# A respaced job plan, a reordered first batch and filler matmuls in a fused attention and gated feed-forward kernel

## The chip, the cores and the metric

The kernel runs on one core of a Trainium2 chip. The metric is the device time of one execution in microseconds (us). The engines are TensorE (PE; its weight loads are PEld), VectorE (DVE), ScalarE (ACT), GpSimd (POOL) and SyncE (SP); SyncE here only issues DMA transposes (its queue is SPq in the profile), and GpSimd also issues the plain DMAs.

## The reference

Two stages, one fed by the other. First an attention over induced points, for each of 4 batches with x of 12416 x 128 and 32 inducing points I:

```python
def mab(q, kv):
    s = scale * (q @ kv.transpose(0, 2, 1))
    s = s - s.max(-1, keepdims=True)
    a = np.exp(s)
    a /= a.sum(-1, keepdims=True) + 1e-09
    return a @ kv
h = mab(I, x)          # (B, 32, 128)
return mab(x, h)       # (B, 12416, 128)
```

Then a gated feed-forward layer on the 49664 rows that come out, with two 128 x 1536 weights and one 1536 x 128:

```python
gate = 1.0 / (1.0 + np.exp(-(x @ w_gate)))
val = x @ w_val
return (gate * val @ w_out).astype(np.float32)
```

## The kernel before, in words

The second attention's output is never formed. Since it is a2 @ h, the kernel computes hw = h @ [w_gate, w_val] once a batch (a 32-row operand for each 128-column piece of the weights) and feeds the weights a2 (32 numbers a token) straight to the products with hw. The sigmoid is taken as tanh, 0.5 * (1 + tanh(z / 2)).

**Blocks.** The main loop (lines 698 to 723) runs over 97 blocks: 24 blocks of 512 tokens for each batch and a last one of the four batches' 128-token tails. A batch's x is cut in 6 chunks q of 2048 tokens, two chunks make a pair d = 0, 1, 2, which serves 8 blocks. A block goes through four steps k. In a step, TensorE fills two value pieces (`v_fill` into the tile "va") and one more ("vb"); VectorE multiplies each with the gate's tanh (`v_mul`, line 434, tiles "u"); TensorE multiplies the u of the step before with w_out (`out_mm`, line 450, tile "acc"). After a block's 12th `out_mm`, in step 0 of the next block, `out_store` copies acc (ScalarE, line 460), transposes it (SyncE's queue, line 462, tile "on") and stores it (GpSimd's queue, line 465).

**Gate pairs.** The gate's 12 pieces go as 6 pairs: `g_next` fills one pair (line 366, tile "g") and takes its tanh on ScalarE (line 421). They run ahead of the multiplies: `gwant` starts at LEADP, rises by one in each step and once more in the odd steps. The first chance of a step stands right behind the va fill, the second behind the vb fill. A pair or a value piece has 32 rows of operand; those named in PADG (pairs) and PADV (value pieces) are spread to 128 rows with zeros (`hw_pad`, GpSimd's copies at lines 259 and 263, tiles "hwp").

**Jobs for the next batch.** In step 2 of a block, in place of the second chance for a pair, `do_extra` runs at most one job, planned by hand with `put(n, ...)`: "s1" (scores of the inducing points for two chunks, and their exp, line 163), "s1t" (the tail's), "h" (a chunk's share of h, line 194 on; VectorE adds it to "hacc" at lines 218 and 220), "hfin" and "hw" (the batch's h and hw), "s2" (scores of a pair d against h). A job's tile comes from the same two-buffer PSUM pool as the gate pairs, and its matmuls stand in TensorE's order ahead of all later fills.

**Events.** `at(n, k, f)` puts work without TensorE at the start of step k of block n: `load_x` (GpSimd's queue, line 84, f32 to f16), `xT_dma` (a chunk's transpose, SyncE's queue, line 142), `a1_dma` (the transpose of an s1 result, line 170, tile "a1n"), and for each s2 job the chain of `rep_events`: `e2_dma` (transpose, line 285), `s2_sum` (GpSimd's row sums, line 302), `s2_rec` (VectorE's reciprocal, line 310), `a2_mul` in two halves (GpSimd, line 320), `rep_dma` in two halves (transposes, line 335, tile "rep"). "rep" is what the value and gate fills of the pair's 8 blocks read, its first half in the first four, its second in the last four.

The order on each engine and queue is the program's order; nothing overtakes. The loads of one batch go into 7 buffers, the x transposes of a batch into one of two large tiles.

**The head.** Batch 0 has no blocks ahead of it, so lines 489 to 561 do its first attention by itself: chunks are transposed on TensorE as they arrive (`xT_pe`, line 480), scored (`s1n_mm`, line 178), passed through exp (line 516) and summed (`h_mm`, lines 194 to 213); then hfin, the scores of the first four token groups, hw, and the first block's rep by way of TensorE (line 550). `warm` (line 139) issues matmuls of 512 columns on ones, whose result nobody reads.

Of the kernel before, what the change touches and what calls it, by code (L numbers as in the profile page):

```python
# [9 lines left out]
F16 = mybir.dt.float16  # L10
AF = mybir.ActivationFunctionType
# [4 lines left out]
P = 128  # L16
# [6 lines left out]
def kernel(  # L23
# [41 lines left out]
    def slot_g(name):  # L65
        return ps_g.tile([P, 2 * TOK], F32, tag="g", name=name)
# [62 lines left out]
    hTs = [pers.tile([P, M], F16, tag=f"hT{b}", name=f"hT_{b}") for b in range(B)]  # L129
    hws = [pers.tile([P, NP2, P], F16, tag=f"hw{b}", name=f"hw_{b}") for b in range(B)]  # L130

    PADG, PADV = (0, 3), (2, 5, 8, 11)
    pads = [pers.tile([P, 8, P], F16, tag=f"hwp{b}", name=f"hwp_{b}") for b in range(B)]
    for t_ in pads:
        nc.gpsimd.memset(t_[:], 0.0)
# [39 lines left out]
    def s1n_mm(ps, b, q, lo, hi):  # L175
        for tk in range(lo, hi):
            j, r = tk % 4, tk // 4
            nc.tensor.matmul(
                ps[:, ds((j * 4 + r) * M, M)], xTs[b][:, ds(q * QT + tk * P, P)], indT[:],
                start=True, stop=True,  # L180
            )
# [10 lines left out]
    def h_mm(ps, b, q, first, last, tail, ch=0, cs=P):  # L192
        for j in range(4):
            nc.tensor.matmul(  # L194
                ps[:, cs:cs + P], ones[:, 0:P], a1n[(b, q)][:, j, :],
                start=first and j == 0, stop=last and j == 3,
            )
            if tail and j == 0:
                nc.tensor.matmul(
                    ps[:, cs:cs + M], ones[:, 0:P], a1n[(b, "t")][:], start=False, stop=False  # L200
                )
        for j in range(4):
            for r in range(4):
                nc.tensor.matmul(
                    ps[r * M:(r + 1) * M, ch:ch + P],
                    a1_chunk(b, q, 4 * r + j),
                    xqs[(b, q)][:, ts(4 * r + j, P)],
                    start=first and j == 0,
                    stop=last and j == 3 and not (tail and r == 0),
                )  # L210
        if tail:
            nc.tensor.matmul(  # L212
                ps[0:M, ch:ch + P], a1n[(b, "t")][:], xtail[:, b, :], start=False, stop=last,
            )
# [23 lines left out]
    def hfin_dve(ps, b):  # L238
        nc.vector.tensor_tensor(out=hTs[b][:], in0=recs[b][:], in1=ps[:, 0:M], op=ALU.mult)
# [235 lines left out]
    def xT_pe(b, q):  # L475
        for half in range(2):
            ps = slot_g(f"xt_{b}_{q}_{half}")
            v = ps[:].bitcast(F16)
            for j in range(8):
                nc.tensor.transpose(  # L480
                    v[:, ts(j, P)], xqs[(b, q)][:, ts(8 * half + j, P)], ident[:]
                )
            dst = xTs[b][:, ds(q * QT + half * 8 * P, 8 * P)]
            if half:
                nc.vector.tensor_copy(out=dst, in_=v[:, 0:8 * P])
            else:
                nc.scalar.copy(out=dst, in_=v[:, 0:8 * P])
# [14 lines left out]
    s1t_exp(0, ps)  # L502

    hps = slot_a("h_0")
    for s in range(NQ + 2):
        if s < NQ:
            xT_pe(0, s)
        if 0 <= s - 2 < NQ:
            q = s - 2
            h_mm(hps, 0, q, q == 0, q == NQ - 1, q == 0, TOK, 0)  # L510
        if 0 <= s - 1 < NQ:
            q = s - 1
            ps = (slot_o if q % 2 else slot_b)(f"s1n_0_{q}")
            an = ep.tile([P, 4, P], F16, tag="a1q", bufs=3, name=f"a1q_0_{q}")
            s1n_mm(ps, 0, q, 0, 16)
            nc.scalar.activation(
                out=an[:].rearrange("p j f -> p (j f)"), in_=ps[:, 0:TOK], func=AF.Exp,
                scale=SCALE,
            )
            a1n[(0, q)] = an  # L520
    nc.scalar.copy(out=haccs[0][:, 0:P], in_=hps[:, TOK:TOK + P])  # L521
    hfin_rec(0, hps[:, 0:P])
    ps = slot_b("hfin_0")
    hfin_mm(ps, 0)
    hfin_dve(ps, 0)

    def q_srcs(b, q, lo, hi):
        return [(hTs[b][:], xTs[b][:, ds(q * QT + t * P, P)]) for t in range(lo, hi)]
# [9 lines left out]
    s2n_exp("q01", ps, 0, 12)  # L538
    hw_pad(0)
    s2n_sum("q00", 0, 4)  # L540
    a2f = ap_.tile([P, 4, M], F16, tag="a2f", name="a2f")
    nc.vector.tensor_tensor(
        out=a2f[:], in0=e2s["q00"][:, 0:4, :],
# [4 lines left out]
    for j in range(4):  # L548
        for g in range(4):
            nc.tensor.transpose(v[g * M:(g + 1) * M, ts(j, P)], a2f[:, j, :], ident[:])  # L550
    rep0 = rep_tile(0, 0)
    nc.vector.tensor_copy(out=rep0[:, 0].rearrange("p j t -> p (j t)"), in_=v[:, 0:TOK])
    s2n_sum("q01", 0, 12)
# [55 lines left out]
    assert ND == 3  # L609
    for b in range(B):  # L610
        n0 = b * BB
        rep_events(n0 + 3, b, 1)
        rep_events(n0 + 10, b, 2)
        nb = b + 1
        if nb < B:
            for e, k0 in enumerate((2, 6, 10)):
                qs = [2 * e, 2 * e + 1]
                for q in qs:
                    at(n0 + k0, 0, load_x, nb, q)
                    at(n0 + k0 + 1, 3, xT_dma, nb, q)  # L620
                if e == 0:
                    at(n0 + k0, 0, load_tail, nb)
                    at(n0 + k0 + 1, 3, xTt_dma, nb)
                put(n0 + k0 + 3, "s1", nb, qs)
                at(n0 + k0 + 4, 1, a1_dma, nb, qs)
                for i, q in enumerate(qs):
                    put(n0 + k0 + 5 + i, "h", nb, q)
# [129 lines left out]
```

## Time and profile before

| | |
|---|---|
| two timed runs | 799.69 and 802.62 us, median 801.15 |
| the profiled execution | 800.62 us, of which the span from the first to the last instruction is 798.8 |
| busy | VectorE 89%, PE 85%, ScalarE 82%, GpSimd 27% of the span |
| mean granted TensorE clock | 0.968 |
| first multiply of block 0 | 32.06 us after the span's start |
| first multiply of block 1 | 44.09 us |

The profile is of one execution. A row of a timeline gives the start, the duration, the engine, the line, the operation, what is written <- what is read, the shapes, how many instructions, and in brackets the idle time before it with what ended it. A row of the waits gives the waiting engine, tile and line, what ended the wait, and the total, the count and the longest in us. A row of the DMA issues gives the size and the median us from issue to landing. A row of a stretch gives busy times by engine, the granted TensorE clock as a share, the mean busy share of the 16 DMA engines and GB/s.

### The profile page before, as it was taken

The numbers are of one execution on the slowest core, as the hardware profiler recorded it, in microseconds if no ns is written. First come the engines' busy times: TensorE is split into PE (matmuls) and PEld (weight loads), VectorE is DVE, ScalarE is ACT, GpSimd is POOL, SyncE is SP. The second block draws the span as 40 slices with busy tenths as digits, with TensorE's granted clock in tenths as the row PEclk, the third lists the DMA queues.
The fourth block names the chain that finished last, engine by engine and source line by source line (L and its number), as shares of the span: only waits on it lengthen the run. The fifth ranks groups of instructions, "written<-read, shape, count | busy, mean of one in ns | idle before, by whom it ended". The sixth has DMA issues, their size and how long they took to land. (4 is left out here: it accounts for less than half of the span.)

```text
span 798.8 us, 12234 instructions
## 1 busy us (share of the span) xinstructions
PE 678.6 (85%) x4518; PEld 249.6 (31%) x4518; DVE 711.0 (89%) x838; ACT 657.0 (82%) x725; POOL 213.9 (27%) x328
## 2 busy tenths in 40 slices
PE   7888799888888869988888869998888888888884
PEld 4322233332333323333333223333333333333332
DVE  2498779999999959999999877999999999999995
ACT  4588779889889859888898867988988988988892
POOL 5232411401601601410341331240160061140001
PEclk9699989999999989999999998999999999999998
DMA  9448849622438496662355694962243243262222
GB/s 180 63 83 153 156 103 159 142 48 54 90 83 161 95 177 106 125 127 53 60 112 100 135 146 98 170 126 58 51 95 82 56 101 84 60 106 60 56 52 53
DMA packets 182300, 80.25 MB, mean 100 GB/s; under 512 B 165952, under 2 KB 166624, under 8 KB 182240
## 3 DMA queue, kind: packets, MB, share of 16 engines
q1 hardware_dynamic: 162112, 40.18, 29.5%
q0 software_dynamic: 20128, 39.30, 22.1%
q8 instruction: 35, 0.57, 0.3%
q14 instruction: 25, 0.20, 0.1%
HBM read 27.80 MB, written 25.43 MB: 67 GB/s over the span
## 5 line engine op out<-in xcount | busy, mean ns | idle before, releaser
L450 PEld LDWEIGHTS <-wo_112 128*128 128x128 f16 x1164 | 108.8, 97 | 175.6 <-issue 94.7
L366 PEld LDWEIGHTS <-hw_159 32*128 32x128 f16 x384 | 14.1, 91 | 60.6 <-issue 60.3
L366 PEld LDWEIGHTS <-hw_162 32*128 32x128 f16 x384 | 14.2, 91 | 57.8 <-issue 57.5
L366 PEld LDWEIGHTS <-hw_161 32*128 32x128 f16 x384 | 13.9, 91 | 56.6 <-issue 56.3
L366 PEld LDWEIGHTS <-hw_160 32*128 32x128 f16 x384 | 14.0, 91 | 54.6 <-issue 54.3
L366 PEld LDWEIGHTS <-hwp_163 128*128 128x128 f16 x192 | 18.7, 99 | 21.4 <-issue 13.6
L366 PEld LDWEIGHTS <-hwp_165 128*128 128x128 f16 x192 | 18.9, 98 | 20.1 <-issue 13.5
L366 PEld LDWEIGHTS <-hwp_164 128*128 128x128 f16 x192 | 18.7, 98 | 19.8 <-issue 13.0
L366 PEld LDWEIGHTS <-hwp_166 128*128 128x128 f16 x192 | 18.6, 97 | 19.2 <-issue 13.3
L194 PEld LDWEIGHTS <-ones 128*128 128x128 f16 x96 | 7.5, 102 | 23.2 <-DMA a1n_0_3473<-e_2_0_3414 6.9
L421 ACT ACTIVATE T_3572<-g_2_3625 128x1024 f16<-128x1024 f32 x1 | 1.0, 1023 | 8.5 <-PE g_2_3625 L366 8.5
L421 ACT ACTIVATE T_5804<-g_2_5857 128x1024 f16<-128x1024 f32 x1 | 1.0, 1023 | 8.1 <-PE g_2_5857 L366 8.1
L421 ACT ACTIVATE T_1340<-g_2_1393 128x1024 f16<-128x1024 f32 x1 | 1.0, 1023 | 6.5 <-PE g_2_1393 L366 6.5
L139 PE MATMUL warm<-ones 128*128 128x512 f16 x16 | 4.9, 477 | 1.5 <-DVE ones L97 1.5
L218 DVE COPY hacc_153<-h_3592 128x256 f32<-128x256 f32 x1 | 0.4, 425 | 6.4 <-PE h_3592 L212 6.4
L194 PE MATMUL h_3592<-a1n_0_3473,ones 128*128 128x128 f16 x4 | 0.6, 296 | 6.4 <-DMA a1n_0_3473<-e_2_0_3414 6.4
L259 POOL COPY hwp_163<-hw_159 32x128 f16<-32x128 f16 x4 | 1.1, 284 | 16.9 <-ACT hw_159 L252 16.7
L194 PE MATMUL h_5824<-a1n_0_5705,ones 128*128 128x128 f16 x4 | 0.6, 297 | 5.8 <-DMA a1n_0_5705<-e_3_0_5646 5.8
L218 DVE COPY hacc_154<-h_5824 128x256 f32<-128x256 f32 x1 | 0.4, 425 | 5.7 <-PE h_5824 L212 5.7
L460 ACT ACTIVATE oT_9504<-acc_9455 128x512 f16<-128x512 f32 x1 | 0.6, 597 | 4.8 <-PE acc_9455 L450 4.8
L188 ACT ACTIVATE a1nt_199<-s1t_197 128x32 f16<-128x32 f32 x1 | 0.2, 197 | 5.3 <-PE s1t_197 L184 5.3
L231 DVE TENSOR_REDUCE hs_559<-h_201 128x32 f32<-128x128 f32 x1 | 0.3, 291 | 4.5 <-ACT hacc_151 L521 4.5
(4133 smaller groups left out, 2764.2 us busy)
## 6 DMA issues: line engine op xcount, KB each, us to landing
xq_0_115<-in_x_dram POOLq DMA_DIRECT2D x1, 512.0 KB, 5.2
xq_1_117<-in_x_dram POOLq DMA_DIRECT2D x1, 512.0 KB, 7.2
xq_2_123<-in_x_dram POOLq DMA_DIRECT2D x1, 512.0 KB, 8.7
xq_3_125<-in_x_dram POOLq DMA_DIRECT2D x1, 512.0 KB, 10.7
xq_4_127<-in_x_dram POOLq DMA_DIRECT2D x1, 512.0 KB, 13.6
xq_5_129<-in_x_dram POOLq DMA_DIRECT2D x1, 512.0 KB, 15.4
xq_0_842<-in_x_dram POOLq DMA_DIRECT2D x1, 512.0 KB, 5.8
xq_1_844<-in_x_dram POOLq DMA_DIRECT2D x1, 512.0 KB, 8.5
```

Of the source, the lines that this page charges most:

```text
L139: nc.tensor.matmul(ps[:, 0:TOK], ones[:, 0:P], ones[:], start=True, stop=True)
L188: nc.scalar.activation(out=an[:], in_=ps[:, 0:M], func=AF.Exp, scale=SCALE)
L194: nc.tensor.matmul(ps[:, cs:cs + P], ones[:, 0:P], a1n[(b, q)][:, j, :], start=first and j == 0, stop=last and j == 3,)
L218: nc.vector.tensor_copy(out=haccs[b][:], in_=ps[:, 0:2 * P])
L231: nc.vector.reduce_sum(out=hs[:], in_=sums.rearrange("p (r m) -> p m r", m=M), axis=AX.X)
L259: nc.gpsimd.tensor_copy(out=pads[b][rows, 2 * i + jj, :], in_=hws[b][rows, p, :])
L366: nc.tensor.matmul(ps[:, ds(col, TOK)], weights(k["b"]), rep[rows, 4 * k["i"] + k["r"]], start=True, stop=True,)
L421: nc.scalar.activation(out=Ts[bi][:, 2 * p:2 * p + 2, 0:T], in_=ps[:].rearrange("p (a t) -> p a t", a=2)[:, :, 0:T], func=AF.Tanh, scale=0.5,)
L450: nc.tensor.matmul(accs[bi][:, 0:T], wo16[:, j, :], u, start=(c == 0), stop=(c == NJ - 1))
L460: nc.scalar.activation(out=oT[:, 0:T], in_=accs[bi][:, 0:T], func=AF.Copy, scale=0.5)
```

## The change

Five edits. (1) The plan of the next batch's loads, transposes and jobs: a table gives each of the three pairs of chunks its own places, the two loads of a pair are a block apart, as are their two transposes, and the whole ends at block 22. With n0 for the batch's first block, before and after (block, step):

| | before | after |
|---|---|---|
| loads of chunks 0 to 5 | 2, 2, 6, 6, 10, 10 (step 0) | 1, 2, 5, 6, 8, 9 (step 0) |
| x transposes | (3,3) x2, (7,3) x2, (11,3) x2 | (2,2), (3,2), (6,2), (7,2), (9,3), (10,2) |
| s1 jobs | 5, 9, 13 | 4, 8, 11 |
| a1n transposes | (6,1), (10,1), (14,1) | (5,2), (9,2), (12,2) |
| h jobs | 7, 8, 11, 12, 15, 16 | 7, 9, 12, 13, 14, 15 |
| s1t, hfin, hw, s2 of the next batch | 6, 17, 18, 19 | 5, 16, 17, 18 |
| s2 of d = 1 | 3 | 2 |

(2) The chain behind each s2 job at n: reciprocal and first multiply from (n+2,1) to (n+2,3), first rep transpose from (n+2,3) to (n+3,0), second multiply from (n+2,3) to (n+3,1), second rep transpose from (n+3,1) to (n+4,0). (3) LEADP from 4 to 3, with PADG from (0, 3) to (2, 5). (4) In the head, the scores of chunk s-1 go ahead of the transposes of chunk s, and h of chunk s-2 behind them; the last scores go ahead of the last two h. (5) Seven `warm` matmuls in the head's last chain: one before and one after hfin, two before the a2 transposes (line 550) and three after them.

```diff
-    PADG, PADV = (0, 3), (2, 5, 8, 11)
+    PADG, PADV = (2, 5), (2, 5, 8, 11)
...
-    for s in range(NQ + 2):
-        if s < NQ:
-            xT_pe(0, s)
-        if 0 <= s - 2 < NQ:
-            q = s - 2
-            h_mm(hps, 0, q, q == 0, q == NQ - 1, q == 0, TOK, 0)
-        if 0 <= s - 1 < NQ:
-            q = s - 1
...
+    for s in range(NQ):
+        if s >= 1:
+            s1n(s - 1)
+        xT_pe(0, s)
+        if s >= 2:
+            h_mm(hps, 0, s - 2, s == 2, False, s == 2, TOK, 0)
+    s1n(NQ - 1)
+    h_mm(hps, 0, NQ - 2, False, False, False, TOK, 0)
+    h_mm(hps, 0, NQ - 1, False, True, False, TOK, 0)
+    psd = slot_g("warm2")
+    warm(psd, 1)
...
     hfin_dve(ps, 0)
+    warm(psd, 1)
...
     s2n_sum("q00", 0, 4)
+    warm(psd, 2)
...
             nc.tensor.transpose(v[g * M:(g + 1) * M, ts(j, P)], a2f[:, j, :], ident[:])
+    warm(psd, 3)
...
-        at(n + 2, 1, s2_rec, b, d)
-        at(n + 2, 1, a2_mul, b, d, 0)
-        at(n + 2, 3, rep_dma, b, d, 0)
-        at(n + 2, 3, a2_mul, b, d, 1)
-        at(n + 3, 1, rep_dma, b, d, 1)
+        at(n + 2, 3, s2_rec, b, d)
+        at(n + 2, 3, a2_mul, b, d, 0)
+        at(n + 3, 0, rep_dma, b, d, 0)
+        at(n + 3, 1, a2_mul, b, d, 1)
+        at(n + 4, 0, rep_dma, b, d, 1)
...
-        rep_events(n0 + 3, b, 1)
+        rep_events(n0 + 2, b, 1)
...
-            for e, k0 in enumerate((2, 6, 10)):
+            plan = (
+                ((1, 0), (2, 0), (2, 2), (3, 2), 4, (5, 2), (7, 9)),
+                ((5, 0), (6, 0), (6, 2), (7, 2), 8, (9, 2), (12, 13)),
+                ((8, 0), (9, 0), (9, 3), (10, 2), 11, (12, 2), (14, 15)),
+            )
+            for e, (l0, l1, x0, x1, s1, a1, hs) in enumerate(plan):
...
-            put(n0 + 6, "s1t", nb)
-            put(n0 + 17, "hfin", nb)
-            put(n0 + 18, "hw", nb)
-            at(n0 + 19, 1, hw_pad, nb)
-            rep_events(n0 + 19, nb, 0)
+            put(n0 + 5, "s1t", nb)
+            put(n0 + 16, "hfin", nb)
+            put(n0 + 17, "hw", nb)
+            at(n0 + 18, 1, hw_pad, nb)
+            rep_events(n0 + 18, nb, 0)
...
-    LEADP = 4
+    LEADP = 3
```

More of the change, by code (lines that the diff above doesn't have):

```diff
@@ L504, with s1n @@
     hps = slot_a("h_0")
-    for s in range(NQ + 2):
-        if s < NQ:
-            xT_pe(0, s)
-        if 0 <= s - 2 < NQ:
-            q = s - 2
-            h_mm(hps, 0, q, q == 0, q == NQ - 1, q == 0, TOK, 0)
-        if 0 <= s - 1 < NQ:
-            q = s - 1
[L513 to L520, printed above, removed]
+    def s1n(q):
+        an = ep.tile([P, 4, P], F16, tag="a1q", bufs=3, name=f"a1q_0_{q}")
+        ps = (slot_o if q % 2 else slot_b)(f"s1n_0_{q}")
+        s1n_mm(ps, 0, q, 0, 16)
+        nc.scalar.activation(
+            out=an[:].rearrange("p j f -> p (j f)"), in_=ps[:, 0:TOK], func=AF.Exp, scale=SCALE,
+        )
+        a1n[(0, q)] = an
+    for s in range(NQ):
[9 more added lines that the diff above has]
+    warm(psd, 1)
     nc.scalar.copy(out=haccs[0][:, 0:P], in_=hps[:, TOK:TOK + P])
@@ L580, in rep_events @@
         at(n + 1, 3, s2_sum, b, d)
-        at(n + 2, 1, s2_rec, b, d)
-        at(n + 2, 1, a2_mul, b, d, 0)
-        at(n + 2, 3, rep_dma, b, d, 0)
-        at(n + 2, 3, a2_mul, b, d, 1)
-        at(n + 3, 1, rep_dma, b, d, 1)
+        at(n + 2, 3, s2_rec, b, d)
+        at(n + 2, 3, a2_mul, b, d, 0)
+        at(n + 3, 1, rep_dma, b, d, 0)
+        at(n + 3, 1, a2_mul, b, d, 1)
+        at(n + 4, 0, rep_dma, b, d, 1)
     def m_mul():
@@ L615 @@
         if nb < B:
-            for e, k0 in enumerate((2, 6, 10)):
+            plan = (
[3 rows of a table added]
+            )
+            for e, (l0, l1, x0, x1, s1, a1, hs) in enumerate(plan):
                 qs = [2 * e, 2 * e + 1]
-                for q in qs:
-                    at(n0 + k0, 0, load_x, nb, q)
-                    at(n0 + k0 + 1, 3, xT_dma, nb, q)
+                for q, lo, xo, h in zip(qs, (l0, l1), (x0, x1), hs):
+                    at(n0 + lo[0], lo[1], load_x, nb, q)
+                    at(n0 + xo[0], xo[1], xT_dma, nb, q)
+                    put(n0 + h, "h", nb, q)
                 if e == 0:
[L622 to L627, printed above, removed]
-            put(n0 + 6, "s1t", nb)
-            put(n0 + 17, "hfin", nb)
-            put(n0 + 18, "hw", nb)
-            at(n0 + 19, 1, hw_pad, nb)
-            rep_events(n0 + 19, nb, 0)
+                    at(n0 + l1[0], l1[1], load_tail, nb)
+                    at(n0 + x1[0], x1[1], xTt_dma, nb)
+                put(n0 + s1, "s1", nb, qs)
+                at(n0 + a1[0], a1[1], a1_dma, nb, qs)
+            put(n0 + 5, "s1t", nb)
[3 more added lines that the diff above has]
+            rep_events(n0 + 18, nb, 0)
         else:
```

## The prediction, made before the changed kernel was run

> **What bounds the kernel now.** I read the page first, then VectorE's busy time by stretches (one stretch per batch of 24 blocks, cut at the start of each batch's first gate-times-value multiply), then VectorE's list of waits, then the timeline around the longest of them, and at last the head.
>
> ```profile
> span 798.8 us, 12234 instructions
> ...
> PE 678.6 (85%) x4518; PEld 249.6 (31%) x4518; DVE 711.0 (89%) x838; ACT 657.0 (82%) x725; POOL 213.9 (27%) x328
> ```
>
> ```profile
> 32.06:44.09 12.03, 8.22 (x10) 0.60 0.17 33
> 44.09:226.97 182.88, 167.21 (x197) 0.97 0.59 114
> 226.97:415.23 188.26, 174.33 (x205) 0.98 0.58 109
> 415.23:605.93 190.70, 174.40 (x206) 0.97 0.58 109
> 605.93:781.91 175.98, 171.49 (x197) 1.00 0.33 70
> ```
>
> Columns: the stretch, its length, VectorE's busy time (and instructions), the granted TensorE clock, the DMA share, GB/s. The first row is block 0, the second batch 0 from block 1 on, then batches 1, 2 and 3. Batch 3 has no next batch to prepare: its 24 blocks take 175.98 us (7.33 each) with VectorE idle for 175.98 - 171.49 = 4.5. VectorE is the bound there. The same subtraction gives 15.7, 13.9 and 16.3 us of idle time in the three batches that prepare the next one. That is what can be won inside the batches; VectorE's busy time stays as it is.
>
> ```profile
> DVE hacc_153 L218 <- PE h_3592 L212: 6.4, 1, 6.4
> DVE hacc_154 L218 <- PE h_5824 L212: 5.7, 1, 5.7
> ...
> DVE hacc_152 L218 <- PE h_1360 L212: 4.2, 1, 4.2
> ...
> DVE rc_1_1132 L310 <- POOL rs_1_1081 L302: 2.1, 1, 2.1
> ```
>
> In each batch VectorE stands at the first "h" job (block 7), and in batch 0 also for 2.1 us at the reciprocal of the d = 1 "s2" job in block 5. Batch 1 shows why:
>
> ```profile
> 272.76 4.05 POOL L320 TENSOR_TENSOR a_1_1_1_3422<-e2n_1_3273,rc_1_3364 128x512 f16<-128x512 f16 x4
> 276.76 0.60 POOL L84 DMA_DIRECT2D xq_2_3447<-in_x_dram  x1
> ...
> 272.82 1.94 SPq L335 DMA_TRANSPOSE rep_1_3420<-a_1_1_0_3366  x1
> 274.87 1.61 SPq L462 DMA_TRANSPOSE on_3469<-oT_3467  x1
> 276.84 6.08 SPq L335 DMA_TRANSPOSE rep_1_3420<-a_1_1_1_3422  x1
> 282.97 4.50 SPq L170 DMA_TRANSPOSE a1n_0_3473<-e_2_0_3414  x1
> ...
> 288.88 2.00 SPq L142 DMA_TRANSPOSE xT_149<-xq_2_3447  x1
> ...
> 289.78 0.29 PE L194 MATMUL h_3592<-a1n_0_3473,ones 128*128 128x128 f16 x1 [6.41 <-DMA a1n_0_3473<-e_2_0_3414]
> ```
>
> ```profile
> xq_2_3447<-in_x_dram POOLq DMA_DIRECT2D x1, 512.0 KB, 5.6
> xq_3_3449<-in_x_dram POOLq DMA_DIRECT2D x1, 512.0 KB, 8.8
> ...
> xT_148<-xq_3_1217 SPq DMA_TRANSPOSE x1, 5.8
> ...
> rep_1_3420<-a_1_1_0_3366 SPq DMA_TRANSPOSE x1, 4.3
> ...
> rep_1_3420<-a_1_1_1_3422 SPq DMA_TRANSPOSE x1, 12.0
> ```
>
> Two loads of x (chunks 2 and 3) start just as the second half of "rep" is issued. The first half landed 4.3 us after issue, the second 12.0 us; its issue held SyncE's queue for 6.08 us instead of 1.94, and the transpose of "a1n" behind it came late for the h job, behind which TensorE, in order, has all later fills.
>
> **The batches, part by part.** *Removed waits.* The a1n transpose moves from event (6,1) to (5,2) while h of the first chunk stays in block 7: two blocks, 14.7 us, instead of some 9. Its own queue time (4.5) and a landing like 12.0 no longer reach the h job. The reciprocal moves from (n+2,1) to (n+2,3), half a block or 3.7 us later, and e2's transpose no longer stands behind two x transposes and the tail's. That wait of 2.1, and its smaller like in the other batches, goes. The other edits to the h, hfin, hw and s2 slots move equal work by a block and cost nothing: the same instructions run in the same slot k = 2 of some block. The second halves of "rep" come later by 0.5 to 0.75 block, but are first read four blocks after the first halves.
>
> If nothing comes in place of these waits, idle time falls to batch 3's 4.5 plus about 0.2 for each of the three added "s1" jobs, so 5.0 (4.8 for the 23 blocks of batch 0): 10.9 + 8.9 + 11.3 = **31.1 us**.
>
> *What is new.* For "rep" the order on GpSimd was: first half's multiply, second half's multiply, out store. Now the out store of block n+2 (event (n+3,0)) lies between the halves, and waits for its transpose, which lies on SyncE behind rep's first half. For the d = 1 rep this is blocks 4 to 7, and x chunks 2 and 3 are loaded and transposed there too, for an s1 job in block 8. I time it from block starts t4, t5, ... 7.33 us apart. The reciprocal is at t4+5.5 (3/4 of a block), the multiply of the first half (4.05, as the second's) ends at t5+2.6; there load 2 and rep's first half start together. SyncE: rep 1.94, then the out transpose at t5+4.5. GpSimd saw on_3469 at
>
> ```profile
> 278.23 0.54 POOL L465 DMA_DIRECT2D out_dram<-on_3469  x1 [0.33 <-issue]
> ```
>
> that is 3.4 us after its issue at 274.87, without a load in flight; with one (5.6) and rep (4.3) ahead I estimate 5.5. So the second multiply starts at t5+7.9 to t5+10 and ends at t6+4.6 to t6+6.7. Then SyncE: rep's second half (1.94 to 6.08), out 1.61, x transpose 2.00, out 1.2 (estimate, under the 1.61), x transpose of chunk 3, landing 5.8 after issue: together 12.6 to 16.7. Chunk 3 is there at t8+2.5 at best (t6 + 4.6 + 12.6, less two blocks) and at t8+8.7 at worst. TensorE wants it at
>
> ```profile
> 627.76 1.22 DVE L434 SCALAR_TENSOR_TENSOR u_0_7625<-T_7574,va_0_7618 128x1024 f16<-128x1024 f16 x1
> ...
> 631.88 0.61 PE L273 MATMUL s_3_7673<-xT_150,hT_158 128*32 128x512 f16 x8
> ```
>
> 4.1 us after a block's start (an s2 job in the same slot). So a **new wait of 0 to 4.6 us in block 8** of each of three batches. I take 2.5, a little over the middle, as one load rather than two goes against each transfer but both loads hit one chain: 7.5 in all. The s1 jobs in blocks 4 and 11 have their transposes issued a block ahead with no rep in the way: x transpose after the out transpose and e2's, some 4.5 us into block 3, plus 5.8, gives t4+3 against t4+4.1, so nothing, at worst 1 us.
>
> By the Trainium skill ("DMA: Bandwidth & Descriptors", Queues, rings and completion order) each DMA engine goes round its queues packet by packet. Half and half, a transpose beside one load would take at most about twice its 4.3 us, 8.6; its issue would then stay near the short end, and with 1 us of wait a batch the sum below would be 766, against 777 with the row's 6.08 each time. The 12.0 beside two loads is close to three shares (12.9), so the trace agrees with the rule; none of its rows has a transpose beside exactly one load.
>
> In batch 0 the first load (0.60 of GpSimd's queue) goes in front of three multiplies for the rep of blocks 5 to 7, which have three blocks to spare: 0.
>
> *Lead.* LEADP 4 to 3 moves every gate pair one slot later; PADG (0,3) to (2,5) keeps the padded pairs in the slots behind the padded value fill, so TensorE's order costs the same. Cover:
>
> ```profile
> 737.37 1.02 ACT L421 ACTIVATE T_8849<-g_3_8885 128x1024 f16<-128x1024 f32 x1
> ...
> 739.94 1.22 DVE L434 SCALAR_TENSOR_TENSOR u_3_8921<-T_8849,va_1_8914 128x1024 f16<-128x1024 f16 x1
> ```
>
> The tanh slot that ends at 738.39 will hold pair 2, which the multiply at 739.94 reads: 1.55 us to spare. So 0.
>
> **The head.**
>
> ```profile
> 19.97 0.62 PE L480 MATMUL xt_5_0_440<-ident,xq_5_129 128*128 128x128 f16 x8 [0.18 <-DMA xq_5_129<-in_x_dram]
> ...
> 21.08 0.69 DVE L485 COPY xT_147<-xt_5_1_450 128x1024 f16<-128x1024 f16 x1 [1.61 <-PE xt_5_1_450 L480]
> ...
> 23.50 0.56 PE L178 MATMUL s1n_5_519<-indT,xT_147 128*128 128x32 f16 x16
> ...
> 24.16 0.60 ACT L516 ACTIVATE a1q_5_520<-s1n_5_519 128x512 f16<-128x512 f32 x1 [1.37 <-PE s1n_5_519 L178]
> ...
> 25.32 0.62 PE L204 MATMUL h_201<-xq_5_129,a1q_5_520 128*32 128x128 f16 x16
> ...
> 29.96 1.01 PE L366 MATMUL g_0_642<-rep_0_628,hwp_163 128*128 128x512 f16 x2 [0.53 <-POOL hwp_163 L259]
> ...
> 41.99 0.39 PE L366 MATMUL g_2_737<-rep_0_628,hw_159 32*128 32x512 f16 x2
> ```
>
> x arrives as before; its last chunk was copied at 21.77, but its scores ran at 23.50, behind h of chunk 4. In the new order they follow the copy: 21.8 + 0.56 + 0.60 + 0.75 for the last h (estimate: 0.62 for its main matmuls and about as much for its ones matmuls at half clock, halved, and some latency) and small gaps give 23.8 instead of 25.94: **2.1 us**. The clock:
>
> ```profile
> 22.00:24.00 2.00, 1.25 (x40) 0.95 (x37) 0.00 (x0) 0.60 (x1) 0.00 (x0) 1.00 1.70 178
> 24.00:25.00 1.00, 0.26 (x6) 0.19 (x3) 0.00 (x0) 0.60 (x1) 0.00 (x0) 0.79 0.60 57
> 25.00:33.00 8.00, 6.10 (x71) 2.60 (x70) 3.64 (x10) 3.73 (x7) 3.20 (x9) 0.50 0.02 3
> 33.00:41.00 8.00, 7.97 (x41) 2.21 (x39) 4.70 (x6) 5.34 (x6) 2.13 (x3) 0.50 0.25 49
> ```
>
> The column after the five engines is the granted clock: 0.50 from 25 to 41 us, after two sparse microseconds. The new order closes those gaps and seven filler matmuls fill the waits behind them, so I expect the clock to stay at 1.00. Then the chain from 25.94 to the first multiply at 32.06 loses 0.6 at the first gate pair (unpadded, 0.39 at full clock, for 1.01) and about 0.3 at the other small matmuls: **0.9**. Block 0 falls from 12.03 to a block's 7.33 plus the row sums of the s2q job, 1.07 (8.22 busy against 171.49/24 = 7.15): 8.4, so **3.6**. The fillers run in TensorE's idle time. Head: 2.1 + 0.9 + 3.6 = **6.6**. The last block and the tail keep their time.
>
> **Sum.** The profiled execution took 800.62 us (span 798.8), 0.5 under the median of 801.15 of the other two. 800.6 - 31.1 + 7.5 - 6.6 = **770.4**.
>
> **Rivals.**
> (a) *No new wait in block 8*: 800.6 - 31.1 - 6.6 = 762.9. For it: DMA share is 0.59 on average; against: the 6.08 issue.
> (b) *The clock falls all the same.* Then the head gains 2.1 and 0.4 (unpadded pair 0.61 instead of 1.01, estimate), and fillers at half clock (0.43 each, half of a pair's) delay: two before the a2 transposes 0.85, three after them 1.3 less the 0.53 that TensorE waited, 0.77; together 1.6, which leaves 0.9. 800.6 - 0.9 - 23.6 (31.1 less 7.5) = 776.1. For it: between 33 and 41 a PE busy 7.97 of 8 us did not bring the clock back, so busy time is not what decides. The Trainium skill ("TensorE: Matmul & The Clock Gate", The HAM clock gate) lets the clock fall after an idle window of about 3.4 us and rise after a busy one as long. By it the clock would not have fallen in this head at all (1.25 of 2 us busy at 22 to 24) and would have risen before 41 us; the trace disagrees with both halves.
> (c) *The jam moves to block 8.* If rep's first half lands like the 12.0, the out store follows at t6+7.7, the second multiply ends at t7+4.9, rep's 6.08 ends at t8+3.7, and chunk 3 lands at t8+14.3: 10 us a batch. 762.9 + 30 = 793.
> (d) *The lead is too short*: slower. If tanh comes later than the 1.55 to spare, each block waits: one queued tanh, a fill and its own tanh (1.02 + 0.39 + 1.02 = 2.43) miss the 1.55 by 0.88, times 96 blocks = 84: 847. It makes the whole slower than before from 0.4 us a block (38/96). Against it: ACT is idle 18% of the span.
> (e) *It doesn't do what it says*: the a1n transpose still lands late, as SyncE waits at rep in (5,0): gain of the head only, 794.
>
> **Chances.** Forecast 0.42, (a) 0.21, (b) 0.20, (c) 0.10, (d) 0.03, (e) 0.04. The range 761 to 785 takes in the forecast, (a) and (b), and the 0-to-4.6 wait (762.9 to 776.7). A measurement here can tell about 2%, 16 us, so faster means under 785: 0.42 + 0.21 + 0.20 and a part of (c): 0.86; same 0.11; slower 0.03.
>
> **What would show it.** Right: VectorE idle in batches 0 to 2 near 7.5 each, no hacc wait over 0.5, no reciprocal wait; the one wait left at an s1 matmul in block 8, ended by the transpose of chunk 3; the first multiply near 29.1 and the next block 8.4 later at clock 1.00. Wrong: a wait elsewhere of more than 2 us per batch; the clock at 0.50 after 25; or blocks longer than 7.4 in batch 3, which would be the lead.

## The result, and the profile after

The changed kernel took 768.12 us (median of 769.95 and 766.30) against 801.15: a ratio of 0.9588, 95% interval 0.9464 to 0.9711. The profiled execution took 769.95 us, span 768.2. The forecast was 770.4, range 761 to 785. One timed run of e1 (2715 us) and one of the kernel before beside it (925 us) lie far outside all others and are left out of every comparison below.

One correction first. The diff in the section on the change has a wrong line: rep's first transpose stands at event (n+3,**1**) in the changed kernel, behind the out store's transpose, and not at (n+3,0). Point (2) of the list there has the same slip, and the prediction's chain for block 8 was worked out for the wrong place. The true lines are

```diff
-        at(n + 2, 3, rep_dma, b, d, 0)
...
+        at(n + 3, 1, rep_dma, b, d, 0)
+        at(n + 3, 1, a2_mul, b, d, 1)
+        at(n + 4, 0, rep_dma, b, d, 1)
```

One of the experiments (e5) runs the order that was costed.

VectorE's time by the same stretches, after (length, VectorE's busy time, clock, DMA share, GB/s):

```profile
29.12:37.93 8.81, 7.97 (x10) 1.00 0.23 45
37.93:211.37 173.44, 166.94 (x198) 1.00 0.68 120
211.37:395.47 184.10, 174.20 (x206) 0.99 0.62 112
395.47:575.17 179.70, 174.07 (x206) 1.00 0.63 115
575.17:751.04 175.87, 171.39 (x198) 1.00 0.32 70
751.04:768.20 17.16, 7.20 (x8) 0.86 0.25 47
```

VectorE's busy time is what it was; its idle time is not. Set beside the forecast's terms (the forecast of a batch is its old length, less its share of the 31.1, plus 2.5):

| stretch | before | forecast | after |
|---|---|---|---|
| to the first multiply | 32.06 | 29.1 | 29.12 |
| block 0 | 12.03 | 8.4 | 8.81 |
| batch 0 from block 1 | 182.88 | 174.5 | 173.44 |
| batch 1 | 188.26 | 181.9 | 184.10 |
| batch 2 | 190.70 | 181.9 | 179.70 |
| batch 3 | 175.98 | 176.0 | 175.87 |
| last block and tail | 16.89 | 16.9 | 17.16 |

The three batches have 6.5 + 9.9 + 5.6 = 22.0 us of idle time, where 7.3 + 7.5 + 7.5 = 22.3 was forecast and 45.9 was there before. VectorE's waits in the changed kernel (in total, times, longest):

```profile
DVE u_9_3725 L434 <- ACT e_2_2_3712 L163: 2.9, 1, 2.9
...
DVE u_9_1493 L434 <- issue: 1.7, 1, 1.7
...
DVE hacc_153 L218 <- PE h_3598 L212: 0.8, 1, 0.8
```

and TensorE's:

```profile
PE s_2_3703 L655 <- DMA xT_149<-xq_3_3460: 2.1, 1, 2.1
...
PE s_1_1471 L655 <- DMA xT_148<-xq_3_1228: 1.4, 1, 1.4
PE h_3598 L194 <- DMA a1n_0_3416<-e_2_0_3332: 1.3, 1, 1.3
```

No reciprocal is in the list any more, and of the h waits one of 0.8 us is left. The two longest outside the head are the forecast ones: the multiply behind the s1 job of block 8, where TensorE waited 2.1 us (batch 1) and 1.4 us (batch 0) for chunk 3's transpose. Block 8 took 9.03, 11.27 and 7.45 us in batches 0 to 2; 7.45 is its length where nothing waits, so it lost 1.6, 3.8 and 0 us. Batch 1 also misses two of the prediction's signs: it has 9.9 us of idle time, not about 7.5, and an hacc wait over 0.5, because the a1n transpose still came 1.3 us late there and made block 7 9.05 us long instead of 7.57.

The head of the changed kernel in order of time (start, length, instruction, the wait ahead of it):

```profile
21.03 0.69 DVE L485 COPY xT_147<-xt_5_1_469 128x1024 f16<-128x1024 f16 x1 [1.61 <-PE xt_5_1_469 L480]
...
21.65 0.56 PE L178 MATMUL s1n_5_500<-indT,xT_147 128*128 128x32 f16 x16
...
23.28 0.41 PE L204 MATMUL h_201<-xq_5_129,a1q_5_499 128*32 128x128 f16 x16
...
27.63 0.39 PE L366 MATMUL g_0_650<-rep_0_636,hw_159 32*128 32x512 f16 x2
...
29.12 1.22 DVE L434 SCALAR_TENSOR_TENSOR u_0_666<-T_653,va_0_659 128x1024 f16<-128x1024 f16 x1 [0.97 <-ACT T_653 L421]
```

and two stretches of it by engine (PE, weight load, VectorE, ScalarE, GpSimd, then clock, DMA share, GB/s):

```profile
25.00:33.00 8.00, 6.54 (x66) 2.49 (x65) 5.51 (x11) 6.41 (x9) 5.33 (x11) 1.00 0.10 20
33.00:41.00 8.00, 6.65 (x53) 2.66 (x52) 7.41 (x10) 6.92 (x9) 1.58 (x2) 1.00 0.34 53
```

The last scores start as the last copy ends, the last h ends at 23.69 (before 25.94, forecast 23.8), the granted clock is 1.00 where it was 0.50, and the first gate pair takes 0.39 us.

### The profile page after: what moved, and what is told of

Read it like the earlier page. It is cut to its first block, busy times and chain, and to the rows that moved or that the text cites. A ratio compares the mean times of both kernels' runs of the same rounds, so it can differ in the third digit from the quotient of the medians.

```text
span 768.2 us, 12231 instructions
## 1 busy us (share of the span) xinstructions
PE 665.9 (87%) x4525; PEld 247.7 (32%) x4525; DVE 709.9 (92%) x838; ACT 656.7 (85%) x725; POOL 214.7 (28%) x328
## 4 chain that ended last, share of the span: by engine, by line
PE 43%; DVE 29%; ACT 16%; DMA 7%; issue 2%; SPq 1%; POOL 1%; POOLq 0%; DVEq 0%; ACTq 0%
DMA xq_4_127<-in_x_dram 2%; DMA a1n_0_3416<-e_2_0_3332 1%; DMA xT_150<-xq_1_5313 1%; SPq L335 1%; DMA xT_148<-xq_1_848 1%; DMA xT_148<-xq_3_1228 1%; DMA xT_149<-xq_3_3460 1%; ACT T_653 L421 0%; ACT T_7945 L421 0%; ACT T_3591 L421 0%; SPq L285 0%; DMA on_9514<-oT_9512 0%; PE acc_1743 L450 0%; PE acc_1650 L450 0%; PE acc_2447 L450 0%
## 5 line engine op out<-in xcount | busy, mean ns | idle before, releaser
L465 POOL DMA_DIRECT2D out_dram<-on_3480 x1 | 0.5, 532 | 15.2 <-DMA on_3480<-oT_3478 15.2
L320 POOL TENSOR_TENSOR a_2_2_0_6354<-e2n_2_6188,rc_2_6352 128x512 f16<-128x512 f16 x4 | 4.1, 1036 | 1.1 <-DVE rc_2_6352 L310 1.1
L320 POOL TENSOR_TENSOR a_1_2_0_4122<-e2n_2_3956,rc_2_4120 128x512 f16<-128x512 f16 x4 | 4.1, 1037 | 1.1 <-DVE rc_2_4120 L310 1.1
L320 POOL TENSOR_TENSOR a_0_2_0_1890<-e2n_2_1724,rc_2_1888 128x512 f16<-128x512 f16 x4 | 4.1, 1036 | 1.1 <-DVE rc_2_1888 L310 1.1
L320 POOL TENSOR_TENSOR a_3_1_0_7785<-e2n_1_7654,rc_1_7783 128x512 f16<-128x512 f16 x4 | 4.1, 1036 | 0.8 <-DVE rc_1_7783 L310 0.8
L320 POOL TENSOR_TENSOR a_2_0_0_4883<-e2n_0_4752,rc_0_4881 128x512 f16<-128x512 f16 x4 | 4.1, 1037 | 0.8 <-DVE rc_0_4881 L310 0.8
L320 POOL TENSOR_TENSOR a_1_0_0_2651<-e2n_0_2520,rc_0_2649 128x512 f16<-128x512 f16 x4 | 4.1, 1037 | 0.8 <-DVE rc_0_2649 L310 0.8
L320 POOL TENSOR_TENSOR a_3_0_0_7115<-e2n_0_6984,rc_0_7113 128x512 f16<-128x512 f16 x4 | 4.1, 1037 | 0.7 <-DVE rc_0_7113 L310 0.7
## 6 DMA issues: line engine op xcount, KB each, us to landing
xq_3_125<-in_x_dram POOLq DMA_DIRECT2D x1, 512.0 KB, 10.5
xq_5_129<-in_x_dram POOLq DMA_DIRECT2D x1, 512.0 KB, 15.3
```

What stands on the lines that cost most here:

```text
L320: nc.gpsimd.tensor_tensor(out=a2[:, r], in0=e2n[:, i, :, r, :].unsqueeze(2).to_broadcast((P, 4, 4, M)), in1=rc[:, i, :, r].unsqueeze(2).un ...
L465: nc.gpsimd.dma_start(out[ds(row0, QT)].rearrange("(p j) c -> p j c", j=QT // P)[:, 4 * k["r"]:4 * k["r"] + 4, :], on[:],)
```

## The experiments

Each kernel is compared with the kernel before on the same chip (797 to 803 us there); "block 8" and the like count from a batch's first block.

### The head: fillers and order

e1, the changed kernel without the fillers:

```diff
-    psd = slot_g("warm2")
-    warm(psd, 1)
...
-    warm(psd, 3)
```

> The changed kernel without its seven filler matmuls. Theory (fillers hold the clock): the granted clock falls to 0.50 in the head as it did before; the first multiply of block 0 stays within 0.7 us of 29.12, block 0 grows from 8.81 to about 12, total about 768 + 4 = 772. Rival (the new order alone holds it, since its last sparse stretch is shorter): the clock stays at 1.00 and the total stays at 768, within 1.

Measured: 764.92 to 770.64 us, ratio 0.9574 (0.9549 to 0.9599). Granted clock and TensorE's busy time, e1:

```profile
24.00:26.00 2.00, 1.44 (x20) 0.81 0.31 30
26.00:28.00 2.00, 1.38 (x34) 0.50 0.03 8
...
34.00:36.00 2.00, 2.00 (x18) 0.63 0.34 66
```

The clock falls, as the theory said, but comes back after some 10 us instead of the 17 of the kernel before, and block 0 takes 10.5 us instead of 12 (8.81 with fillers). The first multiply is at 29.27. So the fillers are worth 1.7 us in this profile, not the 3.2 that the theory gave block 0, and the total does not show it: e9, the changed kernel run again, has a ratio of 0.9567. In the clock the runs differ: its mean is 0.987 to 0.992 in e1 and 0.991 to 0.995 in e9. The theory holds for the clock, though fillers alone do not secure it (e2, e3 and e7 below lose it with all of them in place), and it fails for the price.

e2, the first batch in the old order, fillers kept:

```diff
-    for s in range(NQ):
-        if s >= 1:
-            s1n(s - 1)
-        xT_pe(0, s)
...
+    for s in range(NQ + 2):
+        if s < NQ:
+            xT_pe(0, s)
+        if 0 <= s - 2 < NQ:
...
```

> The changed kernel with the order of scores, transposes and h in the first batch as before, fillers kept. Theory (the order is worth its 2.1 us, the fillers hold the clock): the last h ends near 25.4 instead of 23.6, clock 1.00 from 25 us on, total 770. Rival (order and fillers are both needed): the two gaps of 0.74 us before the last two h come back, the clock falls to 0.50 and block 0 takes 12 us, total 768 + 2 + 1 + 3.5 = 774.5.

Measured: 770.51, ratio 0.9631 (0.9591 to 0.9670). TensorE's last h, e2:

```profile
24.77 0.38 PE L194 MATMUL h<-a1q,ones 128*128 128x128 f16 x4 [0.74 <-ACT a1q L516]
25.08 0.41 PE L204 MATMUL h<-xq,a1q 128*32 128x128 f16 x16
```

Gaps of 0.74 like this one are back and the last h ends at 25.49, 1.8 us later than in the changed kernel. The clock was 0.50 from about 27.2 to 30.6 (0.80 over 26 to 28, 0.50 over 28 to 30, 0.85 over 30 to 32) and 1.00 before and after. The first multiply is at 32.29, 3.2 us late, while block 0 stayed at 8.82. So the order is worth 1.8 us by itself in this profile. Neither side's picture of the clock was right: it fell, but for one short stretch.

### The batches: plan against rep chain

e3 has the old plan of loads, transposes and jobs and the old rep chain, with the new head and LEADP 3:

```diff
-        at(n + 2, 3, s2_rec, b, d)
...
+        at(n + 2, 1, s2_rec, b, d)
...
-            plan = (
...
+            for e, k0 in enumerate((2, 6, 10)):
```

> The changed kernel with the plan of loads, transposes, jobs and rep chains as before; new head and LEADP 3 kept. Theory (the plan is worth 24 us, the head 6.2): 800.6 - 6.2 = 794, h waits of 4 to 6.4 us in block 7 of each batch again. Rival (the shorter lead or the head's earlier finish does part of it): under 790.

e6 has the new plan and the old rep chain:

```diff
-        at(n + 2, 3, s2_rec, b, d)
-        at(n + 2, 3, a2_mul, b, d, 0)
-        at(n + 3, 1, rep_dma, b, d, 0)
-        at(n + 3, 1, a2_mul, b, d, 1)
-        at(n + 4, 0, rep_dma, b, d, 1)
+        at(n + 2, 1, s2_rec, b, d)
+        at(n + 2, 1, a2_mul, b, d, 0)
+        at(n + 2, 3, rep_dma, b, d, 0)
+        at(n + 2, 3, a2_mul, b, d, 1)
+        at(n + 3, 1, rep_dma, b, d, 1)
```

> The changed kernel's plan with the rep chain as before: reciprocal two steps earlier, both multiplies back to back, rep's transposes at (n+2,3) and (n+3,1). Theory (the chain's new places are needed against the reciprocal's wait): waits of 0.5 to 2 us at the reciprocals of d = 1 and d = 2 come back, but rep is done half a block before loads 2 and 3 collide with it, so the waits of block 8 go: total within 3 of 768. Rival (the plan alone removes the reciprocal's wait, since e2's transpose has no two x transposes ahead of it): no reciprocal wait over 0.5, block 8's waits gone, 763.

e12 has the old plan and the new rep chain, with the d = 1 s2 job at block 2:

```diff
-            plan = (
...
+            for e, k0 in enumerate((2, 6, 10)):
+                qs = [2 * e, 2 * e + 1]
+                for q in qs:
+                    at(n0 + k0, 0, load_x, nb, q)
...
```

> The changed kernel with loads, transposes and jobs planned as before, but the new rep chain and the d = 1 s2 job at block 2. Theory (the a1n transpose late behind two loads is the big wait, and only the plan mends it): h waits of 4 us or more in block 7, reciprocal waits gone, total 790 to 794. Rival (the rep chain is the greater part, as the changed plan with the old chain took 787 only): 780 or less.

The four kernels (median in us, 95% interval of the ratio to the kernel before):

| | old rep chain | new rep chain |
|---|---|---|
| old plan | e3: 795.82 (0.9911 to 0.9968) | e12: 780.98 (0.9743 to 0.9794) |
| new plan | e6: 786.95 (0.9767 to 0.9871; 779 to 790) | changed: 764.44 (e9, 0.9535 to 0.9600) |

VectorE's waits in e3 (in total, times, longest):

```profile
DVE hacc L218 <- PE h L212: 16.7, 3, 6.9
...
DVE rc L310 <- POOL rs L302: 9.0, 10, 2.0
```

in e12:

```profile
DVE hacc L218 <- PE h L212: 11.0, 3, 4.1
```

and in e6:

```profile
DVE hacc L218 <- PE h L212: 6.8, 3, 5.9
DVE rc L310 <- POOL rs L302: 5.5, 7, 2.5
```

e3 confirms that the head is worth about 5 us and the rest lies in the batches. The other two were expected wrongly. For e12 the theory said 790 to 794 and the rival 780 or less; it is 781. The rep chain's new places, with the d = 1 s2 job a block earlier than in e3, take 15 us off: the reciprocal waits altogether (9.0 in e3, not in e12's list) and a third of the h waits (16.7 to 11.0). What the s2 job's block has in this was not run by itself. The new plan alone (e6) takes 9, with runs from 779 to 790; its profile is of the fastest of them, so its waits above are the least of the four runs. The longest h wait left is 4.1 us in e12 and 5.9 in e6. In e12 the a1n transpose is late behind two loads and rep's second half. In e6 it is late behind both of rep's halves and two loads that GpSimd issues close together after its two multiplies in a row: in batch 2, where the 5.9 us were lost, at 437.66 and 439.65. With the new plan and the old chain there are waits at the reciprocals, so the plan alone does not remove them. Plan and chain together save 31, 7 more than the 15 and 9 added.

### Block 8: the out store, the loads, the slot

e5 is the order that the prediction costed:

```diff
-        at(n + 3, 1, rep_dma, b, d, 0)
+        at(n + 3, 0, rep_dma, b, d, 0)
```

> The changed kernel with rep's first transpose at event (n+3,0), ahead of the out transpose on SyncE's queue, instead of (n+3,1), behind it. Theory (the prediction's chain: the out store then waits for the transposed out behind rep, so the second multiply starts later, at 7.9 to 10 us into block 5 instead of 5.1, and the second rep transpose with it): the second multiply starts 2 to 5 us later, block 8's wait grows by 1 to 3 us a batch, total 768 + 3 to 9 = 771 to 777. Rival (SyncE's queue is so full there that the order of the two makes no difference): second multiply within 1 us of its place, total within 2 of 768.

Measured: 785.96, ratio 0.9819 (0.9789 to 0.9849); block 8 takes 15.3, 14.5 and 15.2 us. SyncE's queue in batch 1 of e5 (block 5 starts at 254.66, block 8 at 276.78):

```profile
257.20 1.32 SPq L335 DMA_TRANSPOSE rep<-a  x1
258.62 5.12 SPq L462 DMA_TRANSPOSE on<-oT  x1
263.80 1.30 SPq L170 DMA_TRANSPOSE a1n<-e  x1
270.83 4.16 SPq L335 DMA_TRANSPOSE rep<-a  x1
...
282.17 2.65 SPq L142 DMA_TRANSPOSE xT<-xq  x1
```

and GpSimd there:

```profile
266.20 0.53 POOL L465 DMA_DIRECT2D out_dram<-on  x1 [8.48 <-DMA on<-oT]
266.75 4.06 POOL L320 TENSOR_TENSOR a<-e2n,rc 128x512 f16<-128x512 f16 x4
```

The second multiply starts 12.1 us into block 5, chunk 3's transpose is issued 5.4 us into block 8. It is the mechanism of the theory at twice the top of its price (18 us against 3 to 9): GpSimd saw the out transpose, which stands behind rep and beside load 2, only 7.6 us after its issue.

SyncE's queue at the same place in the changed kernel (block 5 starts at 248.10, block 8 at 271.70):

```profile
249.72 1.19 SPq L462 DMA_TRANSPOSE on_3385<-oT_3383  x1
251.01 5.87 SPq L335 DMA_TRANSPOSE rep_1_3388<-a_1_1_0_3340  x1
256.92 2.04 SPq L170 DMA_TRANSPOSE a1n_0_3416<-e_2_0_3332  x1
259.05 8.80 SPq L335 DMA_TRANSPOSE rep_1_3388<-a_1_1_1_3390  x1
...
273.78 2.92 SPq L142 DMA_TRANSPOSE xT_149<-xq_3_3460  x1
```

and GpSimd:

```profile
250.58 0.60 POOL L84 DMA_DIRECT2D xq_2_3365<-in_x_dram  x1
252.67 0.53 POOL L465 DMA_DIRECT2D out_dram<-on_3385  x1 [1.50 <-DMA on_3385<-oT_3383]
253.22 4.06 POOL L320 TENSOR_TENSOR a_1_1_1_3390<-e2n_1_3196,rc_1_3338 128x512 f16<-128x512 f16 x4
257.23 0.60 POOL L84 DMA_DIRECT2D xq_3_3460<-in_x_dram  x1
```

The out transpose goes ahead of both rep and load 2, and GpSimd stores its result 3.0 us after its issue; the second multiply starts 5.1 us into block 5. What is left is the time that three transposes hold SyncE's queue beside the loads, 5.87 + 2.04 + 8.80.

e8 leaves loads 2 and 3 out: the transposes and h of these chunks read chunks 0 and 1 again, so a part of x is not used.

```diff
+                    if e == 1:
+                        at(n0 + lo[0], lo[1], same_x, nb, q)
+                    else:
+                        at(n0 + lo[0], lo[1], load_x, nb, q)
```

> The changed kernel without the loads of chunks 2 and 3 of batches 1 to 3; the transposes and h of these chunks read the tiles of chunks 0 and 1 instead. Theory (a load holds back the transposes beside it by about its own time): rep's two halves and a1n, which landed 9.8, 12.9 and 11.2 us after issue in batch 1, land in 4.3 to 6, SyncE's issues of 5.9 and 8.8 us fall to 2, the waits in blocks 7 and 8 go: 762. Rival (the transposes jam each other on SyncE's queue): issues of 5 us or more remain, and so do half of the waits.

Measured: 762.81, all runs from 762.37 to 763.33. SyncE's queue in batch 1 of e8:

```profile
249.67 1.95 SPq L338 DMA_TRANSPOSE rep<-a  x1
251.66 1.75 SPq L173 DMA_TRANSPOSE a1n<-e  x1
256.04 1.82 SPq L338 DMA_TRANSPOSE rep<-a  x1
```

The times that rep's two halves and a1n held the queue, 5.9, 2.0 and 8.8 us, have become 1.95, 1.75 and 1.82, and no wait is left in blocks 7 and 8. The theory holds: here it is the loads that hold the transposes back, not the transposes each other.

e7 gives the second s1 job a block more:

```diff
-                ((1, 0), (2, 0), (2, 2), (3, 2), 4, (5, 2), (7, 9)),
-                ((5, 0), (6, 0), (6, 2), (7, 2), 8, (9, 2), (12, 13)),
+                ((1, 0), (2, 0), (2, 2), (3, 2), 4, (5, 2), (7, 8)),
+                ((5, 0), (6, 0), (6, 2), (7, 2), 9, (10, 2), (12, 13)),
```

> The changed kernel with the second s1 job in block 9 instead of 8 and the h job of chunk 1 in 8 instead of 9, its a1n transpose from (9,2) to (10,2). Theory (the only thing that comes late for block 8 is chunk 3's transpose, by up to 4 us, and a block's delay covers it): the waits of 1.6 and 3.8 us in block 8 go and nothing comes in their place: 768 - 5.4 = 762.7. Rival (what follows is late by as much: h of chunk 2 in block 12 waits for the later a1n): same total, waits of 2 us or more in block 12.

Measured: 765.78 (763.98 to 768.22), ratio 0.9569 (0.9544 to 0.9593). The batches behave as the theory said: 171.95, 178.85 and 179.69 us, no wait over 0.6, none in block 12. The total is 3 us above the theory. In its profile 1.3 us of this are in block 0, which took 10.08 us because the clock fell with all fillers in place, and 1.3 in the first multiply, which came at 30.40 (the clock was also low from about 19 to 22 us: 0.70 over 18 to 20, 0.50 over 20 to 22).

```profile
30.00:32.00 2.00, 1.48 (x7) 1.00 0.00 0
32.00:34.00 2.00, 1.81 (x8) 0.61 0.33 66
34.00:36.00 2.00, 2.00 (x9) 0.54 0.46 90
```

### The lead

e4:

```diff
-    LEADP = 3
+    LEADP = 4
...
-    PADG, PADV = (2, 5), (2, 5, 8, 11)
+    PADG, PADV = (0, 3), (2, 5, 8, 11)
```

> The changed kernel with LEADP 4 and the padded pairs (0, 3). Theory (the lead costs and brings nothing in the batches, and only the unpadded first pair helps the head, by 0.4): 768.5, block lengths of batch 3 at 7.28 as with lead 3, block 0 up to 1 us longer as one more tanh is taken there. Rival (the lead matters): more than 2 us away in either direction.

Measured: 767.08, ratio 0.9584 (0.9551 to 0.9617), batch 3 at 175.87, block 0 at 9.07. The theory holds within what can be told. One block of its profile stands out: block 4 of batch 0 took 13.4 us, with a wait of 2.5 at a reciprocal and more behind it. The row sums that this reciprocal reads ended at 68.08, where they end at 64.66 in the changed kernel's profile, and e2's transpose ahead of them was issued at 60.55 instead of 57.33. So the chain's half block does not rule out a wait at the reciprocals, though no other profile with the new chain shows one; why SyncE's queue ran late in this run is not known.

### The changed kernel again, and two further steps

e9 is the changed kernel once more.

> The changed kernel again, beside the next ones on one chip: 768, blocks 7 and 8 of batch 1 and block 8 of batch 0 late by 1.5 to 4 us; granted clock 1.00 in the head, or 0.50 for one or two stretches of 3.4 us, since the same instructions of the head lost it from 32.5 to 36 us in one of the runs above and not in others.

e10 joins e7 with an earlier first a1n transpose:

```diff
-                ((1, 0), (2, 0), (2, 2), (3, 2), 4, (5, 2), (7, 9)),
-                ((5, 0), (6, 0), (6, 2), (7, 2), 8, (9, 2), (12, 13)),
+                ((1, 0), (2, 0), (2, 2), (3, 2), 4, (5, 0), (7, 8)),
+                ((5, 0), (6, 0), (6, 2), (7, 2), 9, (10, 2), (12, 13)),
```

> The changed kernel with the second s1 job in block 9 (h of chunk 1 in block 8), and the first a1n transpose at (5,0) instead of (5,2), ahead of rep's first half and load 2's transfer. Theory (what still waits in the batches is the two late transposes of blocks 7 and 8): no wait over 0.7 us left in the batches, batch 0 from block 1 on 172, batches 1 and 2 179 to 179.7 us; 5 to 6 us less than the changed kernel beside it, 762 to 764. Rival (moving a1n up delays rep and with it the x transposes): a wait of 1 us or more in block 9 or 11 and less than 3 us gained.

e11 adds fillers behind the first two gate pairs:

```diff
     g_next()
     g_next()
+    warm(slot_b("warm3"), 4)
     prev = []
```

> As the run before, and four more filler matmuls between the first two gate pairs and the first value fill, where TensorE otherwise waits 0.9 us for the first tanh. Theory (the clock falls where a stretch of some 3.4 us is too thin, wherever its border lies, so thicker is safer): clock 1.00 through the head in nearly every run, mean clock 0.995 or more, 1 to 2 us less than the run before. Rival (the fillers are in the way of the first value fill or the clock was not the matter): same or slower.

| | us, median (range) | ratio to before, 95% | mean clock of the runs |
|---|---|---|---|
| e9 | 764.44 (763.08 to 771.77) | 0.9567 (0.9535 to 0.9600) | 0.991 to 0.995 |
| e10 | 763.63 (761.74 to 764.09) | 0.9538 (0.9516 to 0.9559) | 0.993 to 0.995 |
| e11 | 762.68 (762.43 to 762.73) | 0.9530 (0.9511 to 0.9549) | 0.996 in all |

e9's profile is not the one expected: no h wait, 0.4 us in block 8 of batch 1, none in batch 0. The same place in its queues (block 8 of batch 1 at 268.23):

```profile
249.01 6.02 SPq L335 DMA_TRANSPOSE rep<-a  x1
255.08 2.03 SPq L170 DMA_TRANSPOSE a1n<-e  x1
257.20 4.73 SPq L335 DMA_TRANSPOSE rep<-a  x1
```

With the same instructions the second half of rep holds the queue for 4.73 us, not 8.80, and VectorE's wait in block 8 goes from 2.9 to 0.4. So that wait comes and goes from run to run, and the 22.0 us of idle time above is one sample. Five profiles have this plan and chain: the changed kernel, e1, e2, e4 and e9. Their block 8 of batch 1 is 3.8, 3.3, 4.0, 0.0 and 0.3 us over 7.45. What decides it is open. e10's forecast gain of 5 to 6 us over the changed kernel is not there as a difference of medians (0.8, intervals overlap). Its four runs lie closer together than e9's six, which is as much as so few runs can show. e10's profile has no wait over 0.6 left in the batches, which is the theory's reading; its rival's waits in blocks 9 and 11 are absent. e11's four runs lie within 0.3 us of each other, all under the six of e9, with the clock at 1.00 through its head; against e10 its median gains 0.9 us, and the intervals overlap. It has the lowest median of the kernels that compute everything, though by little.

## Why the prediction was right, and where only by luck

**The batches' waits: right.** The waits at h and at the reciprocals carried the idle time and went: 45.9 to 22.0 us of idle time in the three batches. But the prediction tied the h wait to the plan ("its own queue time (4.5) and a landing like 12.0 no longer reach the h job") and gave the chain only the 2.1 us of the reciprocal and its smaller like. The grid of e3, e6 and e12 shows that the rep chain, with the s2 job's move, does as much as the plan or more (15 against 9 us; the intervals of e12 and e6 overlap). The prediction looked only at a1n's own event. Rep's transposes run through the same queue ahead of a1n, so where they stand moves a1n too.

**Block 8: right in place, 2.5 us a batch against 1.6, 3.8 and 0, and for a wrong reason.** The sum was made for an order that the kernel does not have. For that order (e5) block 8 loses 7.0 to 7.8 us a batch and the total is 786, outside the range of the forecast and between its terms and those of rival (c). The failing step is "with one (5.6) and rep (4.3) ahead I estimate 5.5" for the out transpose, which GpSimd saw after 7.6; the a1n transpose between rep's halves was also left out. In the true order the second multiply starts earlier (5.1 us into block 5 against 7.9 to 10), but rep's two issues took 5.87 and 8.80 where 1.94 and 1.94 to 6.08 were counted. Two errors of opposite sign gave 5.4 us in all against 7.5 forecast, which is luck. And since 8.80 was 4.73 in another run, even the right chain would have given a range of 0 to 4 us a batch and no more.

**The share between queues.** The forecast weighed a rule of the Trainium skill, as half and half between two queues, without a row for one load. The trace after has such rows. In batch 1 the first half of rep was issued 0.4 us behind chunk 2's load, the second half 1.8 us behind chunk 3's (size, us from issue to landing):

```profile
xq_2_3365<-in_x_dram POOLq DMA_DIRECT2D x1, 512.0 KB, 6.4
xq_3_3460<-in_x_dram POOLq DMA_DIRECT2D x1, 512.0 KB, 10.8
...
rep_1_3388<-a_1_1_0_3340 SPq DMA_TRANSPOSE x1, 9.8
...
rep_1_3388<-a_1_1_1_3390 SPq DMA_TRANSPOSE x1, 12.9
```

Rep's first half took 9.8 instead of the 4.3 that it took before without a load, about the load's 5.6 more, while chunk 2's load took 0.8 more than the 5.6 that it had before. In batches 0 and 2 this load took 6.3, and rep's first half 10.6 and 8.5. That is not half and half in time: this load goes nearly through and the transpose waits. The load of chunk 3 fits less well (8.6, 10.8 and 6.7 us in the three batches), and why is open.

The Trainium skill ("DMA: Bandwidth & Descriptors", Queues, rings and completion order) lets each DMA engine go round its queues packet by packet. What shares this would give can be worked out from the totals of the changed kernel's trace (packets, MB, share of the 16 engines' time; the first row is SyncE's queue, the second GpSimd's):

```profile
q1 hardware_dynamic: 162112, 40.18, 32.0%
q0 software_dynamic: 20128, 39.30, 24.2%
```

A packet of SyncE's queue holds some 250 bytes and takes 24 ns, one of GpSimd's some 1950 bytes and 148 ns, both as averages of the whole run. Turn by turn GpSimd would get six sevenths of the time, and a load of 5.6 us would take 6.5 (an estimate from these averages). Chunk 2's 6.3 to 6.4 agree with it. No run here tests the turns themselves.

**The head: right.** Order 2.1 forecast, 1.8 by e2; chain and clock 0.9, of which the first gate pair's 1.01 - 0.39 = 0.62 is in the rows of before and after; block 0 3.6 forecast, 3.2 measured. The clock did stay, in the profile of the changed kernel. But "The new order closes those gaps and seven filler matmuls fill the waits behind them" made it sound safe, and in part it was luck: e7 and e3 lost it at 31 to 36 us with the same head. The cold stretch of the kernel before, 17 us, was five times 3.4; e1's was about three times, e2's one, e3's one, and e7's two were one each. Without the fillers the loss is 1.7 us in block 0, not the 3.6 of rival (b)'s difference.

**The lead: right.** e4 and batch 3 (175.98 before, 175.87 after) show no cost and no gain.

**The rivals.** (a), no new wait, is what e9's profile nearly shows. (b)'s falling clock occurs in some runs, at 1.2 us (block 0 of e3), 1.9 us (e1, head and block 0) or 2.6 us (e7, the same) instead of the 5.7 that lie between (b) and the forecast. (c) is nearly what e5 shows (7.0 to 7.8 us a batch instead of 10). (d) did not happen, and of (e) only the 1.3 us at block 7 of batch 1 did.

## What to carry to other kernels

A late transfer has a queue in front of it: count what the same queue and the same DMA engines hold in the two blocks before, and not only the distance from its issue to its use. Where a load and a transpose share the engines, put the transpose's issue before the load's, or keep a block between them: the out transpose issued ahead of load 2 was seen after 3.0 us, the one behind it (e5) after 7.6. And where the time of one place swings by microseconds from run to run, give it a block of slack: with it (e7, e10) no wait was left there, even if the median hardly moved.

## What the runs showed of the hardware

- Beside the loads of chunks 2 and 3 (512 KB each), the transposes of rep's two halves and a1n held SyncE's queue for 14.8, 16.7 and 12.5 us together in batches 0 to 2 of the changed kernel, and single ones for anything from 1.34 to 8.80. With these loads left out the same three held it for 5.5 together, 1.75 to 1.95 each (e8, batch 1).
- In the head the granted clock was 1.00 or 0.50, but for the stretches at an edge, and its cold spells were some 3.4 us long or a multiple of it: 17 us in the kernel before (24.6 to 41.6), 10 in e1 (25.2 to 35.5), 3.4 in e2 (27.2 to 30.6) and 3.4 in e7 (32.4 to 35.8). The ends are worked out from the shares of the stretches at the edge, those above and, for the kernel before, 0.79 over 24 to 25 and 0.68 over 41 to 42. The Trainium skill ("TensorE: Matmul & The Clock Gate", The HAM clock gate) has a window of that length, free-running. That the same head keeps the clock in one run and loses it in another agrees with it. The same section of the Trainium skill asks for an idle window before a fall. Here no stretch of 3.4 us without matmuls stood ahead of any of these falls (TensorE was busy for 1.25 of the 2 us from 22 to 24 in the kernel before, and for 1.48 of the 2 us before the fall in e7). Another case of the same page of the Trainium skill, short idle gaps between groups of matmuls (A second HAM failure mode: psum-queue depth-cycling), is nearer to what is seen; no run here isolates it.
